# Keys and values in token order "four to a partition" in a windowed attention with a routed expert layer

## The chip, the cores and the metric

The kernel runs on one core of a Trainium2 chip. The metric is the time of one execution on the device in microseconds (us); the median of several runs is compared. The engines are named as the profile names them: PE (TensorE matmuls; PEld its weight loads), DVE (VectorE), ACT (ScalarE), POOL (GpSimd) and SP (SyncE, which here only issues transfers). A "q" behind an engine's name is its instruction queue.

## The reference, cut to what matters

There are 8 batches, 8 heads, 512 local tokens of width 64 and 32 global tokens. A local token sees the 32 global tokens and the local ones within 32 positions; a global token sees all 544. The result, 4352 tokens of 512 numbers, goes through a dense layer of 8 experts whose weights come from a Sinkhorn normalisation.

```python
k_all = np.concatenate([k_g, k_l], axis=2)
out_g = np.matmul(sm(scale * np.matmul(q_g, k_all.transpose(0, 1, 3, 2))), v_all)
mask = np.abs(pos[:, None] - pos[None, :]) <= 32
s_ll = np.where(mask, scale * np.matmul(q_l, k_l.transpose(0, 1, 3, 2)), -1e9)
s_l = np.concatenate([scale * np.matmul(q_l, k_g.transpose(0, 1, 3, 2)), s_ll], axis=-1)
out_l = np.matmul(sm(s_l), np.concatenate([v_g, v_l], axis=2))
...
P = np.exp(logits)                 # logits = x @ w_gate, less their maximum
for _ in range(8):
    P /= P.sum(1, keepdims=True) + 1e-09
    P /= P.sum(0, keepdims=True) + 1e-09
    P *= N / E
for e in range(E):
    out += P[:, e:e + 1] * (np.maximum(x @ w1[e], 0.0) @ w2[e])
```

## The kernel before

**Stages.** The first stage is attention, about the first 265 us; then the Sinkhorn normalisation; then the experts. The order of the instructions on each engine is written out by hand: what the loop emits first runs first on its engine, and each engine works in order. Matmuls of expert 0 are put between the attention's matmuls by `fill(n)`, which takes n pieces from a queue.

**The attention loop** (L429) has 35 iterations. Iteration i works on several head pairs p at once (p counts batch x 4 head pairs; one half batch of four heads is two consecutive p):

- `stage_ak(p = i)` (L282): four PE transposes turn the keys `k16` of two heads into `kTw`, four blocks of 128 tokens, each with 32 global columns, 32 columns of the block on its left and 32 of the block on its right. A DVE copy (L290) takes the transposed keys from PSUM; three POOL copies add the global columns (L291) and the two neighbours' edges (L293, L294).
- `stage_aq(p = i)` (L296): eight PE transposes (L304), four for each head, into two PSUM tiles; ACT copies the first head's rows to `qTz`, DVE the second's (L306). Each head has its own `qTz` whose other 64 rows stay zero.
- `stage_b(p = i - 1)` and `stage_e`: scores (L320, PE), mask and row minimum in one DVE instruction (L324, from PSUM to `st`, with `nm`), exponential on ACT (L334). SP then issues a transposing transfer `uT<-u` (L338), one for each head.
- `stage_c(p = i - 2)`: PE multiplies `uT` with the values, `va` for the block's own tokens (L350) and `vb` for global and neighbouring ones (L351); DVE divides by the row sum (L354, L357).
- `stage_d(p = i - 3)`: transposes back into `xT` (L365, L366).
- In even iterations the 32 global queries of a half batch: `global_scores` (L373, L381, L385) and on POOL `global_norm` (L392, `ug`); in odd ones `global_turn` and `global_out` (L398, L413).

PSUM tiles named `pt` take turns in two buffers, in the order in which they are asked for.

**Token order.** Queries are loaded with four consecutive tokens to a partition (1 KB in a row of the source), so a transposed block holds every fourth token and the copy to `qTz` puts it in order. Keys are loaded block by block, one token to a partition (256 bytes in a row), by four transfers a half batch (`load_k`, L190). Values come one token to a partition too, for two heads by each transfer (`load_va`, L196).

**Who issues which transfer.** POOL issues keys, queries, values and expert weights, and converts fp32 to fp16 on the way. At the end of an even iteration i it issues the keys of two blocks, the queries and values; at the end of an odd one the keys of the other two blocks and values. These are wanted from iteration i + 2 on (`n = i // 2 + 1`, L481). `q16` and `k16` have two buffers. SP issues the edges of `vb` (`load_vb_edges`, L202 and L203, which copy rows of `va` and so wait for its transfers), the global rows of `vb` (L208), the `uT` transfers and, in the first iterations of the second half, some small loads. POOL and SP too work in order: a transfer that waits holds back those behind it.

**The mask** (L229 to L255) is made once: the row order is changed by four transfers to fit the queries' order; three variants serve inner, first and last blocks.

Of the kernel before, what the change touches and what calls it, by code (L numbers as in the profile page):

```python
# [17 lines left out]
P = 128  # L18
NEG = -1.0e9
# [3 lines left out]
def kernel(  # L23
# [124 lines left out]
    with ExitStack() as actx:  # L148
# [24 lines left out]

        def new_qk(k):
            q16 = ain.tile([P, 4, NJ * Dh], FP16, tag="q16", name=f"q16_{k}")
            k16 = ain.tile([P, NJ, 4, Dh], FP16, tag="k16", name=f"k16_{k}")
            qk[k] = (q16, k16)
            return q16, k16

        def q_src(k):  # L180
            b, half = divmod(k, 2)
            return q_l[b, 4 * half : 4 * half + 4].rearrange("h (p s) d -> p h (s d)", s=NJ)

        def k_src(k, so):
            b, half = divmod(k, 2)
            return k_l[b, 4 * half : 4 * half + 4, P * so : P * (so + 1)].rearrange("h p d -> p h d")

        def load_k(k, sos):
            for so in sos:
                nc.gpsimd.dma_start(out=qk[k][1][:, so], in_=k_src(k, so))  # L190

        def load_q(k):
            nc.gpsimd.dma_start(out=qk[k][0], in_=q_src(k))  # L193

        def load_va(b, x):
            nc.gpsimd.dma_start(out=va_buf[b % 2][:, 2 * x : 2 * x + 2, :, 0:Dh].rearrange("p h j d -> p (h j) d"),  # L196
                                in_=v_l[b, 2 * x : 2 * x + 2].rearrange("h (j p) d -> p (h j) d", p=P))

        def load_vb_edges(b, x):
            va, vb = va_buf[b % 2], vb_buf[b % 2]  # L200
            h = slice(4 * x, 4 * x + 4)
            nc.sync.dma_start(out=vb[Sg : Sg + WIN, h, 1:NJ], in_=va[P - WIN : P, h, 0 : NJ - 1])  # L202
            nc.sync.dma_start(out=vb[Sg + WIN : Sg + 2 * WIN, h, 0 : NJ - 1], in_=va[0:WIN, h, 1:NJ])  # L203
# [10 lines left out]
        sk = stage(28, 2).rearrange("p a (b h d) -> p (a b) h d", h=4, d=Dh)  # L214
        sq = stage(30, 2).rearrange("p a (b c) -> p (a b) c", c=NJ * Dh)
# [3 lines left out]
        for so in range(NJ):  # L219
            nc.sync.dma_start(out=sk[:, so], in_=k_src(0, so))  # L220
        nc.scalar.dma_start(out=sq, in_=q_src(0))
# [15 lines left out]
        load_va(0, 0)  # L237
        load_va(0, 1)
# [15 lines left out]
        for s in range(NJ):  # L254
            nc.sync.dma_start(out=mask[Q4 * s : Q4 * (s + 1)], in_=mnat[s:P:NJ])  # L255
# [375 lines left out]
```

## Time and profile before

| | us |
|---|---|
| median of 3 runs (lowest, highest) | 1129.17 (1126.85, 1130.38) |
| profiled execution, its own time | 1128.02 |
| its span | 1126.2 |
| PE busy (share of the span) | 1063.0 (94%) |
| DVE busy | 567.9 (50%) |
| ACT busy | 327.2 (29%) |
| POOL busy | 206.0 (18%) |

The profile's page lists for each engine its busy time, a picture of the span in 40 slices, the chain of waits that ended last, and the costliest groups of instructions. A group's line gives the source line, engine, operation, what is written from what with shapes, how often; then its total busy time and the mean in ns; then the idle time just before it and what ended that. "Issue" lines give transfers, their size and the median time from issue to landing. PE's busy time counts pipelined matmuls and is no measure of its peak. The mean granted clock of TensorE was 0.985 of full speed.

### The profile page before, as it was taken

To read this page: it belongs to the slowest core of one execution; us is meant where nothing else is said; L and a number is where in the kernel's file an instruction comes from. 1 tells how busy PE (TensorE), PEld (TensorE's weight loads), DVE (VectorE), ACT (ScalarE), POOL (GpSimd) and SP (SyncE) were. 2 spreads that over 40 slices of the span, in tenths; PEclk is the share of its full clock that TensorE was granted. 3 is DMA by queue.
4 is the path that set the end of the run, shared out by engine and by line. 5 is a ranking of instruction groups with operands and counts; after the bars stand their busy time and mean duration, and the time that the engine had idled before them with its cause. 6 is when DMAs were issued, how large, how long until landed. Compare 5 with 4: busy or idle time off the path is not lost.

```text
span 1126.2 us, 16517 instructions
## 1 busy us (share of the span) xinstructions
PE 1063.0 (94%) x6394; PEld 539.2 (48%) x6394; DVE 567.9 (50%) x1388; ACT 327.2 (29%) x675; POOL 206.0 (18%) x291
## 2 busy tenths in 40 slices
PE   3598898889999999999999999999999999999998
PEld 2455555555544454445444544445444544454444
DVE  5678787877724444444444444444444444444443
ACT  4466666655421121111111111112111111111111
POOL 6655455541097000000000000000000000000000
PEclk9689999999999999999999999999999999999999
DMA  9999999995102231001300040004000400002222
GB/s 149 158 163 146 130 122 134 134 123 105 18 1 42 34 53 23 1 1 19 57 1 1 1 75 1 1 1 75 1 1 1 76 1 1 1 1 76 75 75 93
DMA packets 181950, 60.97 MB, mean 54 GB/s; under 512 B 156912, under 2 KB 173424, under 8 KB 181872
## 3 DMA queue, kind: packets, MB, share of 16 engines
q0 software_dynamic: 89184, 29.25, 26.9%
q1 hardware_dynamic: 92160, 30.15, 15.6%
q8 instruction: 50, 0.82, 0.3%
q10 hardware_dynamic: 528, 0.52, 0.1%
q14 instruction: 28, 0.23, 0.1%
HBM read 60.57 MB, written 8.91 MB: 62 GB/s over the span
## 4 chain that ended last, share of the span: by engine, by line
PE 82%; DMA 7%; DVE 4%; POOL 3%; issue 2%; ACT 1%; POOLq 0%; DVEq 0%; SPq 0%; ACTq 0%
PE py L115 39%; PE ph L95 38%; DMA k<-in_k_l_dram 4%; DMA uT<-u 2%; POOL k L190 1%; DVE st L324 1%; PE s L320 1%; PE pq L304 1%; POOL va L196 1%; DVE out_nat L123 1%; DMA kgs<-in_k_g_dram 1%; POOL ug L392 0%; PE pog L413 0%; POOL q L193 0%; DVE gm L381 0%
## 5 line engine op out<-in xcount | busy, mean ns | idle before, releaser
L95 PE MATMUL ph<-xT,w1e 128*128 128x512 f16 (+1 forms) x2304 | 500.0, 368 | 0.3 <-DVE P_nat L425 0.3
L115 PE MATMUL py<-w2e,ht 128*128 128x512 f16 x2176 | 497.2, 379 | 0.0
L102 ACT ACTIVATE ht<-ph 128x512 f16<-128x512 f32 (+1 forms) x336 | 192.3, 572 | 687.0 <-PE ph L95 686.5
L95 PEld LDWEIGHTS <-w1e 128*128 128x128 f16 x2304 | 223.1, 98 | 220.5 <-issue 0.9
L115 PEld LDWEIGHTS <-ht 128*128 128x128 f16 x2176 | 210.7, 98 | 232.5 <-ACT ht L102 0.5
L125 DVE SCALAR_TENSOR_TENSOR out_nat<-py,P_nat,out_nat 128x512 f32<-128x512 f32 x238 | 178.7, 751 | 248.1 <-PE py L115 247.2
L104 DVE TENSOR_SCALAR ht<-ph 128x512 f16<-128x512 f32 (+1 forms) x240 | 158.4, 660 | 226.4 <-PE ph L95 225.6
L334 ACT ACTIVATE u<-st,nm 128x224 f16<-128x224 f32 x256 | 105.8, 472 | 55.3 <-DVE nm L324 35.9
L72 POOL DMA_DIRECT2D w1e<-in_moe_w_dram x7 | 5.4, 767 | 510.1 <-PE ph L95 505.0
L324 DVE CUSTOM_DVE_ANT_0 st<-s,mask 128x224 f32<-128x224 f32 x256 | 85.1, 385 | 7.5 <-PE s L320 4.0
L320 PE MATMUL s<-kTw,qTz 128*128 128x224 f16 x256 | 47.8, 275 | 22.6 <-DVE nm L324 19.6
L589 POOL TENSOR_SCALAR out_nat<-out_nat,P_nat 128x512 f32<-128x512 f32 x32 | 49.6, 1561 | 35.7 <-DVE P_nat L586 35.7
L190 POOL DMA_DIRECT2D k<-in_k_l_dram x62 | 47.7, 776 | 0.1
L320 PEld LDWEIGHTS <-qTz 128*128 128x128 f16 x256 | 23.4, 103 | 45.0 <-issue 30.7
L392 POOL TENSOR_SCALAR ug<-ug,gr 128x544 f16<-128x544 f16 x16 | 26.2, 1638 | 29.5 <-DVE gr L391 29.5
L196 POOL DMA_DIRECT2D va<-in_v_l_dram x32 | 29.2, 916 | 0.0
L289 PE MATMUL pk<-identity,k 128*128 128x128 f16 x128 | 16.6, 235 | 11.0 <-DMA k<-in_k_l_dram 10.7
L350 PE MATMUL po<-va,uT 128*128 128x65 f16 x256 | 22.0, 200 | 5.2 <-DMA uT<-u 5.1
L293 POOL COPY kTw<-kTw 128x96 f16<-128x96 f16 x32 | 9.0, 280 | 87.5 <-DVE kTw L290 87.4
L350 PEld LDWEIGHTS <-uT 128*128 128x128 f16 x256 | 19.4, 102 | 9.3 <-DMA uT<-u 5.7
L304 PEld LDWEIGHTS <-q 128*128 128x128 f16 x256 | 19.6, 108 | 7.6 <-issue 1.4
L304 PE MATMUL pq<-identity,q 128*128 128x128 f16 x256 | 22.9, 238 | 0.4 <-DVE kTw L290 0.2
(100 smaller groups left out, 429.6 us busy)
## 6 DMA issues: line engine op xcount, KB each, us to landing
w1e<-in_moe_w_dram POOLq DMA_DIRECT2D x8, 1024.0 KB, 8.0
w2e<-in_moe_w_dram POOLq DMA_DIRECT2D x8, 1024.0 KB, 10.4
out_dram<-out_nat SPq DMA_DIRECT2D x32, 256.0 KB
va<-in_v_l_dram POOLq DMA_DIRECT2D x32, 128.0 KB, 7.5
k<-in_k_l_dram POOLq DMA_DIRECT2D x62, 64.0 KB, 4.9
q<-in_q_l_dram POOLq DMA_DIRECT2D x15, 256.0 KB, 5.9
vb<-va SPq DMA_DIRECT2D x32, 49.5 KB
vb<-vg SPq DMA_DIRECT2D x32, 33.0 KB
```

What stands on the lines that cost most here:

```text
L95: nc.tensor.matmul(ph[:, 0:N], w1e[:, dk, P * fm : P * (fm + 1)], xT[:, dk, P * t0 : P * t0 + N], start=(dk == 0), stop=(dk == DP - 1))
L102: nc.scalar.activation(out=ht[:, 0:N], in_=ph[:, 0:N], func=AF.Relu)
L104: nc.vector.tensor_scalar(out=ht[:, 0:N], in0=ph[:, 0:N], scalar1=0.0, scalar2=None, op0=ALU.max)
L115: nc.tensor.matmul(py, hT[fk][:, P * c : P * (c + 1)], w2e[:, fk, :], start=(fk == 0), stop=(fk == FT - 1))
L125: nc.vector.scalar_tensor_tensor(out=out_nat[:, t, :], in0=py, scalar=P_nat[:, t, e : e + 1], in1=out_nat[:, t, :], op0=ALU.mult, op1=ALU.add)
L190: nc.gpsimd.dma_start(out=qk[k][1][:, so], in_=k_src(k, so))
L304: nc.tensor.transpose(pt[:, s, :], q16[:, c0 : c0 + P], identity)
L320: nc.tensor.matmul(ps[:, jj, 0:KW], qTz[:, P * j : P * (j + 1)], kTw[:, j, :], start=True, stop=True)
L324: nc.vector.tensor_tensor_reduce(out=st[:, jj, :], in0=ps[:, jj, 0:KW], in1=mask[:, mvar[j], :], scale=-scale, scalar=3.0e38, op0=ALU.add, ...
L334: nc.scalar.activation(out=u[:, j, 0:KW], in_=st[:, jj, :], func=AF.Exp, scale=-1.0, bias=nm[:, jj : jj + 1])
L350: nc.tensor.matmul(o, uT[:, 2 * j, :], va[:, 2 * hp + hi, j, 0:W], start=True, stop=False)
L589: eng.tensor_scalar(out=out_nat[:, t, :], in0=out_nat[:, t, :], scalar1=P_nat[:, t, 0:1], scalar2=None, op0=ALU.mult)
```

## The change

Keys are loaded like the queries, four consecutive tokens to a partition, by one transfer a half batch into a raw tile; the queries go into a raw tile too. One iteration later POOL copies both into the order (token within four, head, width). A transposed block of keys then holds every fourth token, and within each block of 128 the columns of `kTw` are kept as four runs of 32; the DVE copy from PSUM, the edge copies, the mask's columns and the rows of `va` and `vb` follow that order. Values therefore come in four transfers a batch, each to 32 partitions and for all eight heads, and the edges of `vb` in four and four transfers of eight partitions. The queries of two heads need only four transposes; ACT makes both copies to `qTz`. Raw and ordered tiles have one buffer each. In the first iterations some work changes place: the first half batch is cast in two parts, all values of batch 0 are loaded ahead of the loop, and `qgP`, `vb` and `vg` are set up in other iterations.

```diff
-        def load_k(k, sos):
-            for so in sos:
-                nc.gpsimd.dma_start(out=qk[k][1][:, so], in_=k_src(k, so))
-        def load_q(k):
-            nc.gpsimd.dma_start(out=qk[k][0], in_=q_src(k))
-        def load_va(b, x):
-            nc.gpsimd.dma_start(out=va_buf[b % 2][:, 2 * x : 2 * x + 2, :, 0:Dh].rearrange("p h j d -> p (h j) d"),
-                                in_=v_l[b, 2 * x : 2 * x + 2].rearrange("h (j p) d -> p (h j) d", p=P))
+        def src_of(x, k):
+            b, half = divmod(k, 2)
+            return x[b, 4 * half : 4 * half + 4].rearrange("h (p s) d -> p h (s d)", s=NJ)
+        def load_qk(k):
+            raws[k] = tuple(ain.tile([P, 4, NJ * Dh], FP16, tag=t, bufs=1, name=f"{t}_{k}") for t in ("qr", "kr"))
+            for dst, x in zip(raws[k], (q_l, k_l)):
+                nc.gpsimd.dma_start(out=dst, in_=src_of(x, k))
+        def order_qk(k):
+            for dst, src in reversed(list(zip(new_qk(k), raws.pop(k)))):
+                nc.gpsimd.tensor_copy(out=dst, in_=src.rearrange("p h (s d) -> p s h d", s=NJ))
+        def load_va(b, s):
+            nc.gpsimd.dma_start(out=va_buf[b % 2][Q4 * s : Q4 * (s + 1), :, :, 0:Dh].rearrange("p h j d -> p (h j) d"),
+                                in_=v_l[b].rearrange("h (j p s) d -> s p (h j) d", p=Q4, s=NJ)[s])
...
+        def load_vb_left(b):
+            va, vb = va_buf[b % 2], vb_buf[b % 2]
+            for s in range(NJ):
+                nc.sync.dma_start(out=vb[Sg + W8 * s : Sg + W8 * (s + 1), :, 1:NJ],
+                                  in_=va[Q4 * (s + 1) - W8 : Q4 * (s + 1), :, 0 : NJ - 1])
...
-            nc.vector.tensor_copy(out=kTw[:, :, 0:P], in_=pt)
+            loc = kTw[:, :, 0:P].rearrange("d j (s p) -> d j s p", s=NJ)
+            nc.vector.tensor_copy(out=loc, in_=pt.rearrange("d s (j p) -> d j s p", j=NJ))
...
-            for hi, copy in ((0, nc.scalar.copy), (1, nc.vector.tensor_copy)):
-                pt = ps_t.tile([P, NJ, P], FP16, tag="pt", name=f"pq{p}_{hi}")
-                for s in range(NJ):
-                    c0 = ((lh + hi) * NJ + s - hi) * Dh
-                    nc.tensor.transpose(pt[:, s, :], q16[:, c0 : c0 + P], identity)
+            pt = ps_t.tile([P, NJ, P], FP16, tag="pt", name=f"pq{p}")
+            for s in range(NJ):
+                nc.tensor.transpose(pt[:, s, :], q16[:, s, lh : lh + 2, :], identity)
+            for hi in range(2):
                 r = slice(Dh * hi, Dh * (hi + 1))
-                copy(out=qTz_buf[2 * (p % NQ) + hi][r].rearrange("d (j s p) -> d j s p", j=NJ, s=NJ),
-                     in_=pt[r].rearrange("d s (j p) -> d j s p", j=NJ))
+                nc.scalar.copy(out=qTz_buf[2 * (p % NQ) + hi][r].rearrange("d (j s p) -> d j s p", j=NJ, s=NJ),
+                               in_=pt[r].rearrange("d s (j p) -> d j s p", j=NJ))
...
                 if i % 2 == 0:
-                    new_qk(n)
-                    load_k(n, (0, 1))
-                    load_q(n)
-                if i == 0 or i % 2 == 1:
-                    load_k(n, (2, 3))
+                    load_qk(n)
+                else:
+                    order_qk(n)
             x, bv = (i + 3) % 4, (i + 3) // 4
...
+            elif bv < B:
+                if x < 2:
+                    load_va(bv, 2 * x)
+                    load_va(bv, 2 * x + 1)
+                    load_vb_globals(bv, (2 * x, 2 * x + 1))
+                elif x == 2:
+                    load_vb_left(bv)
+                else:
+                    load_vb_right(bv)
```

## The prediction

> **What bounds the kernel now.** I read the page's slices first, then stretches of the trace, then the chain in order of time.
>
> ```profile
> PE   3598898889999999999999999999999999999998
> PEclk9689999999999999999999999999999999999999
> DMA  9999999995102231001300040004000400002222
> ```
>
> Each digit is 1/40 of the span, 28 us. From slice 10 on TensorE is full with expert matmuls and the transfers are nearly idle: nothing there is touched. The change lives in the first 265 us, the attention stage, where PE has gaps and the DMA engines are over 90% busy. PE's order is fixed when the kernel is built, so each microsecond that attention ends earlier or later moves the end by as much.
>
> Two consecutive pairs of iterations, by stretches (columns PE, PEld, DVE, ACT, POOL busy, clock, DMA share, GB/s):
>
> ```profile
> 186.40:201.84 15.44, 13.75 (x159) 8.95 (x160) 11.69 (x50) 12.02 (x30) 8.59 (x14) 1.00 1.58 132
> 201.84:216.80 14.96, 13.56 (x152) 8.76 (x153) 13.21 (x52) 8.41 (x21) 8.60 (x14) 1.00 1.45 143
> ```
>
> No engine is full; POOL is at 57%. The waits between 130 and 240 us (seven pairs) say what PE lacks (total, times, longest):
>
> ```profile
> PE pk L289 <- DMA k<-in_k_l_dram: 7.3, 8, 2.5
> PE s L320 <- DVE nm L324: 6.6, 14, 1.0
> ```
>
> Keys landing late cost 7.3/7 = 1.05 us a pair, the scores' lag behind VectorE 0.94. The chain shows why keys are late (start, length, what):
>
> ```profile
> 189.31 0.88 POOL ug L392
> ...
> 190.91 1.57 POOL k L190 x2
> 192.48 0.75 POOL q L193
> 193.23 0.89 POOL va L196
> 194.11 0.30 POOL kTw L291
> ...
> 195.47 6.25 DMA k<-in_k_l_dram
> 201.77 0.23 PE pk L289
> ```
>
> The four key loads of one pair are split over two iterations. The last is issued 4 us after the global normalisation (L392, 1.6 us long, over at 190.95) and lands just before 201.77: 10.8 us from that end.
>
> Prices, from the groups and transfer issues of the same 130:240 stretch:
>
> ```profile
> L291 POOL COPY kTw<-kgT 128x128 f16<-128x128 f16 x13 | 4.4, 335 | 0.0
> L293 POOL COPY kTw<-kTw 128x96 f16<-128x96 f16 x14 | 3.9, 280 | 41.5 <-DVE kTw L290 41.5
> L392 POOL TENSOR_SCALAR ug<-ug,gr 128x544 f16<-128x544 f16 x7 | 11.5, 1637 | 9.5 <-DVE gr L391 9.5
> L306 ACT COPY qTz<-pq 64x512 f16<-64x512 f16 x14 | 8.0, 573 | 8.7 <-PE pq L304 8.7
> L306 DVE COPY qTz<-pq 64x512 f16<-64x512 f16 x14 | 6.0, 428 | 1.0 <-PE pq L304 0.4
> ...
> va<-in_v_l_dram POOLq DMA_DIRECT2D x14, 128.0 KB, 7.9
> q<-in_q_l_dram POOLq DMA_DIRECT2D x7, 256.0 KB, 5.7
> ```
>
> How long is a pair? The transposes of iterations 7 and 31 (L289) start at 68.7 and 255.1 us: 24 iterations, 12 pairs, 15.5 us each.
>
> **The change part by part.**
>
> *Keys and queries: load, then reorder on GpSimd.* Removed per pair: four key issues (0.78 us each). Added: one key issue of the queries' shape (0.76 us) and two POOL copies of 128x1024 fp16. No such copy is in the trace. The nearest rows are POOL's own copies: 335 ns for 128 elements and 280 for 96 give 1.72 ns an element, hence T = 335 + 896 x 1.72 = 1.9 us. The low end: the mask's affine selects in the first 10 us, 212 ns for 32 elements and 293 for 128 (0.84 ns each), give 1.05 us. The high end is the rate of L392, 3.0 ns: 3.1 us. I take 1.9, by the same operation's rows.
>
> Counted from the end of L392: queries issue (0.76), keys issue, keys land 5.7 us after, so 6.5. That is the queries' row; those stood behind two short-packet key loads, the keys will stand behind the queries. Ends: 4.4 us, the queries' shortest, and 7.9, the values' row. I take the row of the same shape. The keys are copied at 6.5 + 1.9 = 8.4, where the old keys came at 10.8 and PE asked for them at 9.75. The wait goes, with 1.35 us to spare: -1.05 a pair. Queries are copied at 10.3. PE asked at 202.89, 11.9 after; less the lost wait that is 10.9: hidden by 0.6 us. What is late next is the scores' wait on VectorE, which stays.
>
> *What queues behind the waiting copy on POOL.* It waits for the landing; behind it stand the value loads (every second pair, 2 x 0.92), the three window copies of the next iteration (0.66 from start to end at 194.07) and L392, which releases the next load. So a new loop exists: 0.76 + 5.7 + 2 x 1.9 + 0.66 + 1.64 = 12.6 us, 14.4 with value loads, 13.5 on average. Pairs will last about 14.2, so every second one can lose a little: +0.2 a pair. Single buffers for ordered and raw tiles make the copy wait for the former transposes too; those are over by 195 us, before the landing.
>
> *Query transposes.* Four instead of eight an iteration. Eight take 202.89 to 203.34 on PE, 0.45 us, so 0.45 a pair less work; PE also stands 0.94 a pair waiting for VectorE, so I count -0.25 (ends 0 and -0.45).
>
> *Copies.* DVE loses 2 x 0.43 a pair, ACT gains 2 x 0.57: from (12.02 + 8.41)/2 = 10.2 to 11.4 of some 14 us. What hides it is ACT's wait for these transposes (8.7 us in seven pairs); uncovered it would cost 1.15 x 12 = 14 us. The gain on DVE I count at nothing (to -0.86 a pair). Window copies with shorter runs and the key copy in another order (L306's 428 ns has that pattern; L290 took 420) cost 0.0 to 0.1 us a pair on POOL and DVE: hidden in POOL's slack, +1 us in all if not.
>
> *Values in four quarters of 32 partitions, edges in eight issues instead of four a batch.* SP issues 4 x 0.59 = 2.4 us more in a batch's 31 us, and it waits for the last quarter with the score transposes (L338) queued behind it; stage C on PE needs those. Now SP loses 11.4 us in the seven pairs to such waits and PE doesn't wait for uT between 80 and 260 us. Hidden; without cover 2.4 x 7 batches = 17 us.
>
> *Start.* The mask gets three more small DVE copies (at most 0.6 us by the 0.57 us copy at 6.37); its transfer starts at 9.98, DVE is done at 7.1: hidden. Two value loads move into POOL's 2.7 us idle before 10.5, three key issues go, so the q_g load, which is in the chain (18.49, 4.09 us), can start up to 4 us earlier; but it then stands behind more value bytes, and 17 us of uT waits follow at 34.7 to 54.6. Weights issued behind a reorder at iterations 3 and 5 come some 7 us later; L115 first needs them at 76 us. I take -1, ends -4 and +2.
>
> Sum: 12 x (-1.05 - 0.25 + 0.2) - 1 = -14 us. The profiled run took 1128.0 (span 1126.2): 1114. The median of the runs is 1.2 above it: **1115 us**.
>
> *Two rules against the trace.* POOL's short copies run at 1.72 ns an element here. The Trainium skill, GPSIMD Engine Reference, "Elementwise — side-by-side cycle accounting", has 1.8 cycles an element at 1.2 GHz for a tight one-input loop and 2.6 for two inputs: an estimate of 1.5 to 2.2 us for T; at 2.2 the loop averages 14.1, 15.0 with value loads; the 0.2 becomes 0.6 and the sum -9. Second, POOL's 96-element copies last 266 to 298 ns from 60 to 260 us, whatever DVE does. SBUF — State Buffer, "Who interferes with whom", speaks against long POOL copies: a DVE instruction that uses both of its ports shuts GpSimd out for its whole length. In this stage DVE reads PSUM, which that rule leaves free; if it applied, an estimate of up to 0.7 us (xn's length) for each reorder would add 1.4 a pair and make the sum +3.
>
> **The rivals.**
>
> 1. *GpSimd's loop becomes the bound (slower).* The copies run at L392's rate, 3.1 us. Then queries are ready at 6.5 + 6.2 = 12.7, 1.8 after PE asks, and the loop is 0.76 + 5.7 + 6.2 + 0.92 + 0.66 + 1.64 = 15.9 on average, 16.8 with value loads: +0.4 a pair, or +1.3 if short pairs can't make up for long ones, 12 x 0.4 to 12 x 1.3: 1133 to 1144. It decides where the landing and two copies together pass 11.5 us, which brings the loop to 15.5: T = 2.9 at a landing of 5.7, T = 1.8 at 7.9. For it: L392, the only long POOL arithmetic here. Against it: the short copies' slope, and fewer packets in the queue.
> 2. *Everything is hidden and the copies are fast* (T near 1.1). The loop is 12 us, the wait and all of the 0.45 go, and DVE's lighter load shortens the scores' wait by 0.2: 12 x -1.7 - 2 = -22: 1107. For it: the affine selects' slope. Against: DVE stands between matmuls anyway.
> 3. *Score transposes come late.* SP's longer wait and eight edges take uT's slack; PE waits 2 to 2.4 us a batch: -14 + 15 = about +1: 1130. For it: SP stands before L338 now. Against: no uT wait in 180 us.
> 4. *ACT takes the wait's place*: half of the 14 us uncovered gives -7: 1122.
>
> **How the numbers follow.** Forecast 0.42, rival 2 0.18, rival 4 0.14, rival 3 0.07 (half of it within 0.3%), rival 1 0.19. A difference under 0.3% (3.4 us) can't be told from none. Faster: 0.42 + 0.18 + 0.13 = 0.73, less 0.02 for mixtures: 0.71. Same: 0.06. Slower: 0.23. The forecast's own range is 1109 to 1121. For 8 in 10: down to 1104, below rival 2, and up to 1136, into rival 1's lower half.
>
> **What would show it.** Right: no wait of pk on a key transfer; POOL's 128x1024 copies under 2.5 us; pairs of 14 to 14.4 us; q0's packets fewer by a third; ACT's query copies twice as many. Wrong: pq or pk waiting for POOL, window copies late before L320, L350 waiting for uT, or VectorE's lag growing beyond 0.94 a pair.

## The result and the profile after

| | before | after |
|---|---|---|
| median (lowest, highest), us | 1130.35 (1126.85, 1132.79) | 1143.01 (1132.38, 1147.5) |
| ratio of after to before | | 1.0108, 95% interval 1.0085 to 1.0131 |
| profiled execution, us | 1128.02 | 1136.88 |
| its span, us | 1126.2 | 1135.1 |

The change makes the kernel about 12 us slower; 1115 was forecast, and 1143 lies outside the range. Only the attention stage moves: the key transposes of iterations 7 and 31 start 186.4 us apart before and 196.1 after, so a pair of iterations takes 16.3 us instead of 15.5, and these 9.7 us are more than the 8.9 us between the spans.

The page of after: the slices, queue q0, what the engines' costliest groups waited for, and the loads.

```profile
PE   3587888779999999999999999999999999999997
...
DMA  9999999993300413000400040004000400002222
...
q0 software_dynamic: 64368, 29.11, 21.6%
...
PE 80%; DMA 13%; DVE 3%; ACT 2%; issue 1%; SPq 1%; POOL 0%; DVEq 0%; ACTq 0%; POOLq 0%
...
L363 PE MATMUL po<-va,uT 128*128 128x65 f16 x256 | 23.8, 200 | 35.8 <-DMA uT<-u 35.7
...
L191 POOL COPY k<-kr 128x1024 f16<-128x1024 f16 x15 | 15.6, 1040 | 51.8 <-DMA kr<-in_k_l_dram 47.8
...
va<-in_v_l_dram POOLq DMA_DIRECT2D x32, 128.0 KB, 5.2
qr<-in_q_l_dram POOLq DMA_DIRECT2D x15, 256.0 KB, 5.2
kr<-in_k_l_dram POOLq DMA_DIRECT2D x15, 256.0 KB, 6.7
```

Much of what was forecast happened: q0 has 28% fewer packets, GpSimd's copies take 1.04 us, no key transpose on PE waits for a transfer. But the chain now holds 13% of transfers (7% before), and the value matmuls on PE, which waited 5.1 us for `uT` in the whole run before, wait 35.7.

The waits of the same stretch as in the prediction, 130 to 240 us, PE's first:

```profile
PEld L363 <- DMA uT<-u: 14.1, 9, 3.6
PE po L363 <- DMA uT<-u: 12.9, 8, 3.5
...
PE s L333 <- DVE nm L337: 4.5, 9, 1.6
```

No pk line with a key transfer is left (7.3 us before); in its place stand 12.9 us of the value matmuls waiting for `uT`, a wait that before did not have here at all. SP's queue:

```profile
SPq L351 <- ACT u L347: 48.1, 16, 5.8
SPq L351 <- ACT qTz L319: 12.0, 7, 2.1
...
SPq L202 <- DMA va<-in_v_l_dram: 0.6, 1, 0.6
```

SP no longer waits for values (0.6, before 11.4); the score transposes (L351) wait for ScalarE's exponentials, and in 7 of them the last thing in front was a query copy. From 60 to 280 us, by line, the weight loads and the products of after's value matmuls (counted together, though the waits of the two overlap) stood idle for `uT`:

```profile
  DMA uT<-u: 51.9, 30
```

Before it was 0.2. The page's stretch by pairs (iterations 18 to 23; columns as in the prediction):

```profile
157.76:173.44 15.68, 13.07 (x151) 8.48 (x150) 10.97 (x49) 12.88 (x30) 8.18 (x13) 1.00 1.20 120
173.44:188.30 14.86, 12.68 (x135) 8.10 (x134) 12.02 (x50) 9.88 (x23) 8.26 (x13) 1.00 1.05 137
188.30:204.71 16.41, 13.06 (x151) 8.47 (x149) 10.89 (x49) 12.88 (x29) 8.18 (x13) 1.00 1.35 124
```

PE is busy for 12.9 us of a pair on average, 0.7 less than in the two pairs shown before, and yet the pairs are longer (15.65 against 15.2 us). The chain of after from 162 us on shows what fills them:

```profile
162.42 0.37 ACT u L347
162.80 0.03 issue
162.82 13.21 DMA uT<-u x2
176.03 0.47 ACT qTz L319
176.50 0.02 issue
176.52 0.58 ACT qTz L319
177.10 0.03 issue
177.13 0.86 ACT u L347 x2
177.99 0.02 issue
178.01 6.42 DMA uT<-u
184.43 0.05 issue
184.48 0.20 PE po L363
```

Two query copies, the last exponentials, a transfer of 6.4 us, the value matmuls: a chain in which PE only comes at the end. GpSimd's order of time in the same place:

```profile
160.82 1.64 POOL L405 TENSOR_SCALAR ug<-ug,gr 128x544 f16<-128x544 f16 x1 [0.81 <-DVE gr L404]
162.42 0.82 POOL L187 DMA_DIRECT2D qr<-in_q_l_dram  x1
163.24 0.76 POOL L187 DMA_DIRECT2D kr<-in_k_l_dram  x1
163.99 1.57 POOL L194 DMA_DIRECT2D va<-in_v_l_dram  x2
```

SP issues the even iteration's second `uT` in between, and PE needs it in the odd iteration that follows, where the waits stand:

```profile
162.82 1.23 SPq L351 DMA_TRANSPOSE uT<-u  x1
```

Within 3.2 us, 512 KB of queries and keys and two value loads are queued, and the first of them ahead of that `uT`. Before, at the same place (iteration 22), the order was the other one: the first keys were queued at 190.91, and `uT` had gone out 0.9 us earlier:

```profile
189.97 1.24 SPq L338 DMA_TRANSPOSE uT<-u  x1
```

**How far uT was from being late.** A `uT` transfer adds to its semaphore sixteen times, and it has landed with the last of these: the 6.42 us from 178.01 in the chain above are such a flight. The trace also holds single packets, 1024 of 256 bytes in queue q1 for each `uT`, in the order of issue, so the first can be told. Means over the nine even iterations 12 to 28 for the second head, in us from the iteration's first key transpose (where PE waited for the landing, the value matmul started 0.05 us after it):

| kernel | issued | flight | landed | first head's value matmuls | second head's | PE's wait there |
|---|---|---|---|---|---|---|
| before | 4.71 | 2.90 | 7.61 | 11.54 | 11.78 | 0 |
| after | 4.79 | 7.42 | 12.21 | 9.88 | 12.26 | 1.97 |

PE wants the second head 0.24 us after the first. So before, PE asked at 11.78 for what was there at 7.61: a slack of 4.2 us. After, PE asks at 10.12, 1.66 us earlier, mostly because the iteration lost its key wait and half of its query transposes: that is the gain itself. The landing is 4.6 us later. The two together, 6.3, are 2.1 more than the slack, and PE waits 2.0. Of the longer flight 1.95 us are the time to the first packet (1.21 to 3.16), 2.6 the time from there to the landing (1.69 to 4.26). In the odd iterations it was the other way round: there the second head's flight was 7.96 us before, with only 0.89 us of slack, and is 5.52 after, with 2.95.

**What moved is the loads.** SP issues that `uT` as late as before (4.79 against 4.71). But before, all nine went out 0.8 to 1.3 us ahead of the first load of their iteration (1.04 on average), and landed after 2.7 to 2.9 us, one after 3.95. After, all nine go out 0.4 to 1.0 us behind it (0.69), and land after 6.4 to 9.1. The loads stand behind the normalisation (`ug`), and that waits for a reciprocal on VectorE (`gr`) which stood right behind VectorE's query copy. Without that copy the reciprocal is over at 2.39 us instead of 4.04, and all that GpSimd does behind it comes earlier too.

### The profile page after: what moved, and what is told of

Same layout as the page of the kernel before. It is cut to its first block, busy times and chain, and to the rows that moved or that the text cites. A ratio compares the mean times of both kernels' runs of the same rounds, so it can differ in the third digit from the quotient of the medians.

```text
span 1135.1 us, 16317 instructions
## 1 busy us (share of the span) xinstructions
PE 1055.6 (93%) x6266; PEld 532.8 (47%) x6266; DVE 555.2 (49%) x1361; ACT 348.3 (31%) x708; POOL 198.9 (18%) x274
## 3 DMA queue, kind: packets, MB, share of 16 engines
q1 hardware_dynamic: 90576, 30.15, 15.5%
## 4 chain that ended last, share of the span: by engine, by line
PE 80%; DMA 13%; DVE 3%; ACT 2%; issue 1%; SPq 1%; POOL 0%; DVEq 0%; ACTq 0%; POOLq 0%
PE ph L95 38%; PE py L115 38%; DMA uT<-u 11%; ACT u L347 1%; DMA va<-in_v_l_dram 1%; PE s L333 1%; DVE st L337 1%; ACT qTz L319 1%; DVE gm L394 1%; DMA out_nat<-in_v_g_dram 1%; PE po L363 1%; PE sa L386 0%; PE po L364 0%; SPq L202 0%; DMA mask<-out_nat 0%
## 5 line engine op out<-in xcount | busy, mean ns | idle before, releaser
L363 PE MATMUL po<-va,uT 128*128 128x65 f16 x256 | 23.8, 200 | 35.8 <-DMA uT<-u 35.7
L600 POOL TENSOR_SCALAR out_nat<-out_nat,P_nat 128x512 f32<-128x512 f32 x32 | 49.6, 1561 | 35.7 <-DVE P_nat L597 35.7
L319 ACT COPY qTz<-pq 64x512 f16<-64x512 f16 x64 | 36.9, 576 | 14.0 <-PE pq L316 13.2
L367 DVE RECIPROCAL rc<-po 128x8 f32<-128x8 f32 x32 | 6.6, 206 | 51.0 <-PE po L364 51.0
L194 POOL DMA_DIRECT2D va<-in_v_l_dram x32 | 25.1, 792 | 2.8 <-PE s L333 2.2
L191 POOL COPY k<-kr 128x1024 f16<-128x1024 f16 x15 | 15.6, 1040 | 51.8 <-DMA kr<-in_k_l_dram 47.8
L364 PE MATMUL po<-vb,uT 128*128 128x65 f16 x256 | 23.8, 199 | 0.0
L370 DVE TENSOR_TENSOR xn<-po,rc 128x512 f16<-128x512 f32 x32 | 22.1, 691 | 1.1
```

What stands on the lines that cost most here:

```text
L319: nc.scalar.copy(out=qTz_buf[2 * (p % NQ) + hi][r].rearrange("d (j s p) -> d j s p", j=NJ, s=NJ), in_=pt[r].rearrange("d s (j p) -> d j s ...
L363: nc.tensor.matmul(o, uT[:, 2 * j, :], va[:, 2 * hp + hi, j, 0:W], start=True, stop=False)
L600: eng.tensor_scalar(out=out_nat[:, t, :], in0=out_nat[:, t, :], scalar1=P_nat[:, t, 0:1], scalar2=None, op0=ALU.mult)
```

## The experiments

Ratios are to the kernel before, run beside it on the same chip; one point is 1% (11.3 us). The changed kernel stands at +1.1 points.

| run | from | edit | median, us | ratio (95%) |
|---|---|---|---|---|
| e1 | after | second query copy on VectorE | 1126.77 | 0.9972 (0.9952 to 0.9993) |
| e2 | after | both loads moved to the odd iteration | 1129.05 | 0.9964 (0.9947 to 0.9981) |
| e3 | after | no GpSimd copies, loads write the order | 1145.51 | 1.0131 (1.0091 to 1.0171) |
| e4 | after | four more edge transfers a batch | 1159.66 | 1.0233 (1.0192 to 1.0274) |
| e5 | after | last exponentials ahead of the query copies | 1126.24 | 0.9967 (0.9932 to 1.0002) |
| e6 | after | e2 and e1 | 1121.0 | 0.9898 (0.9863 to 0.9932) |
| e7 | after | e2 and e5 | 1115.68 | 0.9848 (0.981 to 0.9886) |
| e9 | after | edges issued by GpSimd | 1138.01 | 1.01 (1.0055 to 1.0145) |
| e10 | after | e2, e5 and e1 | 1143.25 | 1.0137 (1.0107 to 1.0166) |
| b1 | before | both query copies on ScalarE | 1133.62 | 1.0024 (1.0001 to 1.0047) |
| b2 | before | all key loads at the even iteration's end | 1127.03 | 0.9981 (0.9959 to 1.0003) |
| b3 | before | b1 and b2 | 1129.81 | 0.9978 (0.9954 to 1.0003) |
| f1 | after | values and edges as before | 1137.45 | 1.0101 (1.0059 to 1.0142) |
| f2 | before | values and edges as after | 1134.12 | 1.0062 (1.0031 to 1.0094) |
| f3 | before | b3 and f2 | 1136.69 | 1.0075 (1.004 to 1.0109) |
| f4 | after | no GpSimd copies, raw tiles read | 1148.24 | 1.0193 (1.0154 to 1.0232) |
| f5 | after | each load in four parts | 1129.18 | 1.0007 (0.9975 to 1.0039) |
| f6 | after | e5, and the keys' load alone moved | 1117.15 | 0.9892 (0.9858 to 0.9926) |

### ScalarE's copies, the moment of the loads, the packets (e1, e2, e3, b1)

```diff
# e1
-                nc.scalar.copy(out=qTz_buf[2 * (p % NQ) + hi][r]...
+                (nc.scalar.copy, nc.vector.tensor_copy)[hi](out=qTz_buf[2 * (p % NQ) + hi][r]...
# e2
-                if i % 2 == 0:
+                if i == 0:
                     load_qk(n)
-                else:
+                elif i % 2 == 1:
                     order_qk(n)
+                    if n + 1 < 2 * B:
+                        load_qk(n + 1)
# e3: q16 and k16 with two buffers, no order_qk
+                src = x[b, 4 * half : 4 * half + 4].rearrange("h (p s) d -> p s h d", s=NJ)
+                nc.gpsimd.dma_start(out=dst, in_=src)
# b1, in the kernel before
-            for hi, copy in ((0, nc.scalar.copy), (1, nc.vector.tensor_copy)):
+            for hi, copy in ((0, nc.scalar.copy), (1, nc.scalar.copy)):
```

> The changed kernel with one thing undone: the second head's query copy is back on VectorE. After the change PE waits for uT at the start of stage C (PE and its weight loads name uT in 30 waits between 60 and 280 us; 12.9 us of PE time in seven pairs) and ScalarE makes its two query copies (0.58 us each) just before the last exponentials that release the transfer. Theory ACT (the second copy makes uT late): each of the 32 transfers goes 0.58 us earlier, the wait in odd iterations falls by about as much, some 9 us in all: about 1134. Theory BURST (the transfer is slow because query and key loads are issued at the same moment): the wait hardly falls, VectorE's work grows by 0.43 us an iteration: 1140 to 1146. Theory SP (edge issues hold the queue): unchanged, 1143.

> The changed kernel with the query and key loads of the next half batch issued at the end of odd iterations, right behind the reorder that frees the raw tiles, instead of at the end of even ones. Theory BURST: the second head's transfer of even iterations (issued at 162.8, landed 6.8 us later, where the old kernel's comparable ones took about 2.4 us) no longer meets the loads and lands in 3 us or so; the iteration from the odd key transposes to the even ones falls from about 8.9 back towards 7.5 us, 16 times 1.4 = 22 us: 1118 to 1125. Theory ACT: the issue is as late as before, the time stays within 4 us of 1143. Theory SP: the same, 1143.

> The changed kernel without the reorder on GpSimd: the loads of queries and keys at the end of even iterations write the ordered tiles directly (two buffers each), in runs of 64 numbers, so 256-byte reads and 128-byte writes instead of 1024 and 512, four times as many packets. Theory BURST with long packets (a transfer's packets take turns with the load's, and a 512-byte packet holds an engine about twice as long as a 128-byte one): a transposing transfer beside the burst lands in about 4.5 instead of 6.8 us and the time falls to 1128 to 1136. Theory BURST by sheer load time (four times the packets, some 5 us of all engines for each half batch instead of 2.5): the wait stays or grows, 1143 to 1160. Theory ACT or SP: 1143.

> The kernel before with one part of the change alone: both query copies on ScalarE (still eight transposes in two PSUM tiles). Theory ACT: uT goes 0.58 us later in each iteration, and the old kernel has little slack there, so stage C begins to wait for uT: 1134 to 1140 against 1130. Theory BURST or SP: hidden, within 3 us of 1130, as the prediction counted it.

e1 and e2 each take back 1.4 points, and both part `uT` from the loads. In e2 the even iteration's second `uT` flies 5.16 us instead of 7.42: 2.8 to 4.7 where nothing is queued beside it, and still 6.4 to 8.4 in the four iterations that queue two value loads 0.4 us ahead of it. e2 misses the 1118 to 1125 us of its theory by 4 us. e1 is faster than all three of its theories expected, and not by an earlier issue: `uT` goes out at 4.84 us, as late as in after. VectorE's copy holds the reciprocal back to 3.86 us, the first load is queued 0.8 us behind `uT` on average, and the flight is 5.04, beside an even iteration that is 0.7 us longer. In the kernel before, both copies on ScalarE (b1) cost a quarter of a point: that `uT` is issued 0.66 us later (5.37), now 0.3 us behind the first load, and flies 4.65, still inside the slack. e3 has the burst and the copies with 256-byte reads, and no reordering on GpSimd: 1.3 points slower than before, flight 6.50 us, 51.2 us of `uT` waits from 60 to 280 us. Long packets are not needed for the loss.

### Edges, and the exponentials first (e4, e5, e6, e7)

```diff
# e4
                 elif x == 2:
                     load_vb_left(bv)
+                    load_vb_left(bv)
# e5 (e7 has this and e2's edit; e6 has e1's and e2's)
             fill(1)
+            if Bs:
+                stage_e(pb, 1, 1)
             if A:
                 stage_aq(pa)
             if ks is not None:
                 global_norm(ks, gsu.pop(ks))
             fill(1)
-            if Bs:
-                stage_e(pb, 1, 1)
```

> The changed kernel with the four left-edge transfers of each batch issued twice: 4 x 0.78 = 3.1 us more on SP's queue a batch (0.78 is the step between two of them in the changed kernel's chain), ahead of the transposing transfers of the next even iteration. Theory SP (the extra edge issues make uT late): seven batches times up to 3.1 = 22 us more, 1155 to 1165. Theories ACT and BURST: SP mostly waits for ScalarE's exponentials (some 60 of 110 us), so at most a third of it shows: 1143 to 1150.

> The changed kernel with one change of order: the last exponentials of the second head stand ahead of the query transposes and of ScalarE's two query copies, so uT goes out about 1.2 us earlier. With the second copy back on VectorE alone (0.58 us earlier) the time fell from 1143 to 1127. Theory ACT, refined (what counts is how late uT is issued against a landing time of 2.3 to 8 us): 1.2 us earlier gives as much or more, 1114 to 1127. Theory BURST: the transfer still meets the loads unless it gets out ahead of them; at most half of it, 1130 to 1143. Third possibility, that VectorE's or ScalarE's load and not the order made the difference in that run: no change, 1143.

> The changed kernel with both single steps together: loads at the end of odd iterations, second query copy back on VectorE. Alone they gave 1129 and 1127. If they are two separate causes of the same wait (a late issue and a slow landing), they add until the wait is gone: of 40 us of uT waits in the changed kernel some 30 go, 1110 to 1120. If both do the same thing, that is keep the transfer and the loads apart in time, they don't add: 1124 to 1130.

> The changed kernel with loads at the end of odd iterations and the last exponentials ahead of the query copies; both copies stay on ScalarE. If the uT wait is all that the change cost, what is left is the gain that was forecast for the rest (no wait for keys, four transposes fewer): 1108 to 1118. If ScalarE's added 1.2 us an iteration pair costs something of its own, 1120 or more.

Four more edge issues a batch (0.77 us each on SP) cost 1.25 points, 14 us: once the slack is gone, what stands on SP ahead of `uT` is paid. (In e4's profile the granted clock between 80 and 280 us was 0.92, in after's 0.98, so a part of the 14 us may be slower matmuls.) e5 issues the even iteration's second `uT` at 4.18 instead of 4.79 us and gains 1.4 points. It shows both orders in one kernel: in iterations 14, 18, 22 and 26 `uT` now goes out 0.8 us ahead of the first load and lands after 2.7 to 4.0 us; in the other five the load is still 0.4 to 1.6 us ahead, and it takes 7.2 to 8.0. With the loads moved as well (e7) the time is 1115.7 us, 1.5 points faster than before, and 2.6% faster than the changed kernel (0.9848 / 1.0108 = 0.974). From iteration 12 on its pairs take 14.2 us (15.7 before, 16.3 after), and the waits between 130 and 240 us begin with

```profile
POOL kTw L308 <- DVE kTw L303: 39.6, 15, 4.9
ACT u L347 <- DVE nm L337: 11.2, 11, 1.8
...
PE s L333 <- ACT qTz L319: 4.4, 7, 0.8
PE s L333 <- DVE nm L337: 4.3, 8, 1.0
```

with PE waiting for VectorE and the query copies, and only once, for 1.3 us, for `uT`. Everything that the forecast counted on is in this kernel. (Over iterations 7 to 31 its pairs take 14.7 us, where the forecast's sum had 14.4.) e6, which puts the second copy on VectorE instead, is half a point behind, 1 us above its expected range: VectorE waits 11.0 us for ScalarE's copy in the same stretch.

### What three edits together do, the edges on another queue, the burst in the old kernel (e9, e10, b2, b3)

```diff
# e9, in both edge functions
-                nc.sync.dma_start(out=vb[...
+                nc.gpsimd.dma_start(out=vb[...
# b2
-                    load_k(n, (0, 1))
+                    load_k(n, range(NJ))
                     load_q(n)
-                if i == 0 or i % 2 == 1:
-                    load_k(n, (2, 3))
```

> The changed kernel with all edge transfers of vb issued on GpSimd's queue instead of SP's, in the same places of the program. Four edges issued in a row hold SP for 3.1 us; issuing four more a batch cost 17 us in the run with doubled edges. Theory SP (the eight edge issues a batch, ahead of the transposing transfers, carry a good part of the loss): uT goes up to 3 us earlier in two of four iterations, and the time falls by 8 to 17 us, 1126 to 1135, although GpSimd now spends some 6.4 us more a batch. If the edges cost only where their number passes SP's slack, which eight do not: 1140 to 1150.

> The changed kernel with loads at the end of odd iterations, the last exponentials ahead of the query transposes, and the second query copy on VectorE. With the first two alone 1115.7 was measured; there scores now wait for ScalarE's query copies (13 us in 15 waits of PE). If those waits are on the path, halving them gives 1108 to 1113. If VectorE's 0.43 us an iteration is worth as much (its lag behind the scores is the other wait that is left), 1114 to 1121.

> The kernel before with one part of the change's timing alone: all four key loads of a half batch are issued at the end of the even iteration, with the queries and values, in the old packets and the old token order. The wait of pk on keys (about 1.05 us a pair) must go, since the last key load is issued some 4 us earlier: -12 us if nothing takes its place, 1118. Theory BURST (loads at that moment slow the second head's transfer of even iterations): uT waits of 1 to 2 us appear in odd iterations and eat the gain, 1126 to 1136. If the long packets are needed for that: 1116 to 1122.

> The kernel before, with both suspected causes put in and nothing else of the change: both query copies on ScalarE (0.24% slower alone) and all four key loads together with the queries at the end of the even iteration (0.19% faster alone, where the key wait, worth some 12 us, went and 17 us of waits for uT came). Eight query transposes, the old value loads and the four old edges stay, GpSimd copies nothing. Theory (uT is late because it is issued behind ScalarE's copies and flies beside the burst): the two add up or worse, 1134 to 1145 us, with over 25 us of waits of PE for uT in the whole span and most of them in odd iterations. Rival (the loss in the changed kernel needs its value loads, edges or GpSimd copies): 1127 to 1132 us, under 20 us of waits for uT.

Taking the edges off SP gains 0.1 point, less than the interval, and 1138.0 us lies between its two expected ranges; what the edges cost on GpSimd instead isn't told apart. e10 was to be the best and is 2.9 points worse than e7. Between 130 and 240 us PE has no wait for `uT` there; the waits show another engine:

```profile
DVE qTz L319 <- ACT qTz L319: 19.1, 13, 2.0
...
POOL ug L405 <- DVE gr L404: 17.6, 6, 3.0
PE s L333 <- DVE nm L337: 15.3, 13, 1.9
```

VectorE's copy and ScalarE's read the same PSUM tile and run one after the other. With the exponentials ahead of ScalarE's copy, VectorE stands up to 2.0 us for it, and the scores, the key transposes and the normalisation stand behind VectorE. The change's one tile for both heads thus makes ScalarE for both copies the better choice, once `uT` has slack.

b2 is the old kernel with the burst. The key wait is gone, 13.1 us of `uT` waits appear between 60 and 280 us, and 0.2 points are left, an interval that still reaches no gain. b3 has burst and copies and, against the theory, costs nothing either: 19.5 us of such waits, and no key wait. So the two suspects alone do not rebuild the loss. In b3 the second `uT` is issued at 4.90, 0.8 us behind the first load, and still flies only 4.86 us, not 7.42; PE asks at 11.2, not 10.1. Two questions followed: what else of the change lengthens the flight, and whether values, edges or GpSimd's copies do it.

### Values, edges and GpSimd's copies (f1, f2, f3, f4)

```diff
# f1: after, with load_va(b, x), load_vb_edges(b, x) and their places in the loop as before
# f2: before, with load_va(b, s), load_vb_left, load_vb_right and their places as after
# f3: f2 with the edits of b1 and b2
# f4: after, raw tiles with two buffers
+            qk[k] = tuple(t_.rearrange("p h (s d) -> p h s d", s=NJ) for t_ in raws[k])
...
-                else:
-                    order_qk(n)
```

> The changed kernel, but values and edges are loaded as before: one transfer of two heads in each iteration, four edge transfers a batch (the rows of the values are then not in the order of the scores' columns; the work is the same). Theory V (the new value loads and edges are what makes the burst and ScalarE's copies cost more here than in the kernel before): 1118 to 1129 us, under 30 us of waits for uT between 60 and 280 us (51.9 in the changed kernel). Rival C (GpSimd's copies are): still 1137 to 1146 us and over 40 us of such waits.

> The kernel before with the new value loads and edges alone: quarters of 32 partitions, two in every first and second iteration of four, and four and four edge transfers (rows not in the order of the scores' columns; the work is the same). Theory V: slower, 1134 to 1148 us, with over 15 us of waits for uT between 60 and 280 us (0.2 before). Rival C: 1126 to 1132 us.

> The kernel before with all three: new value loads and edges, both query copies on ScalarE, all key loads at the end of the even iteration (rows of the values not in the order of the scores' columns; the work is the same). The former run with the last two alone took 1129.8 us with 19.5 us of waits for uT between 60 and 280 us. Theory V: 1140 to 1155 us, over 40 us of such waits. Rival C: 1128 to 1133 us.

> The changed kernel without GpSimd's two copies a pair: the transposes read 128 neighbouring columns of the raw tiles, which have two buffers (the reordering of keys and queries is left out, the work of the other engines is the same). Theory V: 1137 to 1147 us, over 40 us of waits for uT. Rival C: 1118 to 1130 us, under 30 us of them.

Neither theory holds. With the old values and edges the changed kernel loses as much (f1: 46.0 us of `uT` waits, flight 7.07). The new ones cost the kernel before 0.6 points (f2), and 1.0 on top of b3 (f3), with only 4.8 and 25.4 us of `uT` waits. In f2 the flight of the even iterations is no longer than before (2.73) and PE waits for keys there, 8.8 us between 130 and 240; how the new value loads make its pairs longer was not followed further. In f4 the transposes read two runs of 64 columns in the raw tiles, not 128 neighbouring ones as its expectation has it, so the order is kept; `uT` waits are 54.1 us. Without GpSimd's copies the changed kernel is 0.9 points slower, not faster: nothing then holds the value loads of the odd iteration back until the keys have landed. That this is why was not tested.

### The rate at which loads are queued (f5, f6)

b3 and f1 differ in how the same bytes are queued: by their rows the four key loads and the queries take GpSimd 3.9 us to issue (2 x 1.57 and 0.76), the two whole loads 1.6.

```diff
# f5
-            for dst, x in zip(raws[k], (q_l, k_l)):
-                nc.gpsimd.dma_start(out=dst, in_=src_of(x, k))
+            for h in range(4):
+                for dst, x in zip(raws[k], (q_l, k_l)):
+                    nc.gpsimd.dma_start(out=dst[:, h], in_=src_of(x, k)[:, h])
# f6: e5's edit, and
+                if i == 0:
+                    load_raw(n, "kr", k_l)
                 if i % 2 == 0:
-                    load_qk(n)
+                    load_raw(n, "qr", q_l)
                 else:
                     order_qk(n)
+                    if n + 1 < 2 * B:
+                        load_raw(n + 1, "kr", k_l)
```

> The changed kernel with each of the two loads of a pair issued in four parts of one head (64 KB each, the same bytes and packets, eight issues of some 0.76 us in place of two). In the changed kernel the second head's uT of an even iteration is issued 4.8 us after that iteration's first key transpose, as before (4.7), but flies 6.3 us (3.7 before); in the kernel before with the four key loads and the queries behind one another it flew 4.5. Theory (what slows uT is that two transfers of 256 KB are queued within 1.5 us): that flight falls under 5.2 us and the waits for uT between 60 and 280 us under 40 us; keys land later, so 1128 to 1142 us. Rival (it is the long packets, or something other than the rate of issue): flight still 5.8 us or more, waits over 46 us, 1140 us or more.

> The changed kernel with the last two exponentials ahead of ScalarE's query copies, and the burst parted: the keys' load moves to the end of the odd iteration behind GpSimd's copies, the queries' stays at the end of the even one. Theory (two 256 KB transfers at once slow uT): each is harmless by itself, under 12 us of waits for uT between 60 and 280 us, 1108 to 1116 us, at least as fast as with both loads moved (1115.7). Rival (any load issued there is as bad): over 20 us of waits, 1120 to 1128 us.

f5 changes nothing but the number of issues: the same bytes, packets, copies and edges. Its GpSimd in order of time, at the same place:

```profile
160.44 0.61 POOL L188 DMA_DIRECT2D qr<-in_q_l_dram  x1
161.06 0.55 POOL L188 DMA_DIRECT2D kr<-in_k_l_dram  x1
...
164.20 0.59 POOL L188 DMA_DIRECT2D kr<-in_k_l_dram  x1
164.72 1.65 POOL L195 DMA_DIRECT2D va<-in_v_l_dram  x2
```

The eight parts take 4.3 us to queue (the three flights that f5's expectation compares, 6.3, 3.7 and 4.5, are 7.42, 2.90 and 4.86 to the landing), and the value matmuls' waits for `uT` from 60 to 280 us fall to

```profile
  DMA uT<-u: 13.6, 9
```

The even iteration's second `uT` flies 4.80 us, its first packet comes after 1.60 us, although the first part is queued 0.4 us ahead of it on average. The kernel is 1.0 points faster than the changed one, although its key transposes now wait for GpSimd (5.2 us between 130 and 240, where the keys' last part lands later). The expected time and flight are met, and the rival's are not. Each part is also smaller than a whole load, so f5 shows what parting does and not whether size or spacing does it. f6 parts the burst in two places: flight 3.92 us and pairs of 14.0 us from iteration 12 on. One load alone is not harmless: queued within 0.4 us of `uT` it makes it 4.2 to 5.7 us, queued 0.8 us behind it 2.7 to 3.7. At 1117.15 us it misses its expected range by 1 us, and its 16.3 us of `uT` waits are above the 12 expected; its time agrees with e7's within the intervals.

In the table the first load is counted from the issue of `uT` (negative: ahead of it); e2 and e7 queue only value loads there, in four of the nine iterations.

| kernel | issued | first load | flight | landed | PE's wait there | pair, iterations 12 to 29 |
|---|---|---|---|---|---|---|
| before | 4.71 | 1.04 | 2.90 | 7.61 | 0 | 15.7 |
| b3 | 4.90 | -0.79 | 4.86 | 9.76 | 0 | 15.2 |
| after | 4.79 | -0.69 | 7.42 | 12.21 | 1.97 | 16.3 |
| f5 | 4.64 | -0.44 | 4.80 | 9.44 | 0.08 | 14.9 |
| e5 | 4.18 | -0.08 | 5.59 | 9.78 | 0.83 | 15.1 |
| e2 | 4.78 | -0.40 | 5.16 | 9.94 | 0.75 | 15.5 |
| f6 | 3.66 | 0.44 | 3.92 | 7.57 | 0 | 14.0 |
| e7 | 3.58 | 0.81 | 4.42 | 8.00 | 0.15 | 14.2 |

The order at the issue is not all: in e7 the four with value loads 0.8 us behind them still take 4.5 to 8.1 us. Why was not followed.

## Why the prediction was wrong

*The gains were there.* The key wait of 1.05 us a pair went in full. The even iteration, from its first key transpose to the next, fell from 7.91 to 6.74 us in after, as the sum of key wait and query transposes asks; in f6 and e7 the odd one fell too, from 7.81 to 7.3 and 7.4. With `uT` freed by two edits (e7) the kernel takes 1115.7 us; the forecast was 1115. That the two agree so closely is partly luck: the exponentials' new place is none of the change's parts, and whether it would speed up the kernel before was not run.

*T, the copy of 128x1024, was taken at 1.9 us and is 1.04.* The mask's selects (0.84 ns an element) were the right neighbours, not POOL's own short copies. By the rows of after, 270 ns for 96 elements and 1040 for 1024, the fixed part of such a copy is 190 ns and an element takes 0.83 ns; the slope between two short copies of different kind had made it 1.72. The prediction's estimate from the Trainium skill, GPSIMD Engine Reference, "Elementwise — side-by-side cycle accounting", 1.5 us at the least, was too high as well: the measurement decides. The rule on VectorE's ports (SBUF — State Buffer, "Who interferes with whom") shows in no row: after's copies of keys and queries average 1040 and 1041 ns between 130 and 240 us.

*The landing was taken at 5.7 and is 6.7 for the keys,* inside its ends. With the smaller T the reorder is still in time, and the GpSimd loop, the +0.2 and rival 1, never bound.

*The start* was taken as -1: the transposes of iteration 7 start at 67.7 instead of 68.5 us.

*The step that failed is "PE doesn't wait for uT between 80 and 260 us. Hidden; without cover 2.4 x 7 batches = 17 us",* and with it the copies' "What hides it is ACT's wait for these transposes". Both named a cover and neither measured how thick it was. A wait of nothing says only that the slack is not below zero; the trace gives it as 4.2 us for the second head of the even iterations. The forecast gain alone takes 1.66 of that, since PE comes to `uT` earlier while SP issues it as late as before (4.79 against 4.71 us). What was left, 2.5 us, was overspent by a term that was not in the sum at all: the effect of the new loads on someone else's transfer. The prediction priced when queries and keys land and nothing that flies beside them, although the change moves the loads of a pair from 1.0 us behind the even iteration's second `uT` to 0.7 us ahead of it. That flight grew by 4.5 us. A part of the move comes from a term that was put at nothing, "The gain on DVE I count at nothing": the copy that VectorE lost had held back the normalisation and with it the loads, and e1, which gives it back, has the loads 0.8 us behind `uT` again. f5 shows the loads' part: the same loads, queued over 4.3 us instead of 1.6, bring the flight to 4.8 us and give back 1.0 points.

*What it costs in the sum:* 2.0 us of wait in each pair, 24 us over 12 pairs. With that the sum of -14 becomes +10; the profiled executions differ by +9, the medians by +13. From iteration 12 on the pairs of f6 and e7 are 2.2 and 2.0 us shorter than after's, 24 to 27 us over 12 such pairs; their medians are 26 and 27 us lower.

*The copies on ScalarE* cost a quarter of a point in the kernel before (b1), and the second of them 1.4 in the changed one (e1). The price of 14 us "uncovered" was near in size, but not as time of ScalarE: the copies stand ahead of the exponentials that release `uT` (e5), and without the copy on VectorE the loads come earlier. The cover was the slack of `uT`, not ScalarE's wait for the transposes.

*The edges on SP* gain 0.1 point when GpSimd issues them (e9), so they were hidden or nearly so, unless GpSimd lost what SP gained. Four more of them cost 14 us (e4), near the 17 for no cover.

*The rivals.* Rival 3 had the place right, score transposes late, and its mechanism wrong: SP's edges were to eat the slack, at 1130 us with a chance of 0.07. Rival 4 had ScalarE's share. Rival 2 comes nearest to e7 in mechanism (fast copies, all hidden) but its 1107 us was not reached. Rival 1 has the result in its range, 1133 to 1144, by luck: its loop does not exist.

*What stays open.* The slack is shared, so its users' prices don't add: f5, e2, e5 and e1 alone each give back 1.0 to 1.4 points, e2 and e5 together 2.6. Why the new value loads and edges slow the kernel before (f2), and why the changed kernel is slower without GpSimd's copies (f4), was not settled.

## What to carry to other kernels

Before a step is costed at nothing because nobody waits for it, measure its slack: the time from landing to first use, in every phase of the loop, less what the change itself takes by making the consumer come earlier. When loads are moved or merged, or an engine that releases them is relieved, ask which transfer that something waits for starts in the same microseconds, whether it goes out ahead of the loads or behind them, and price that one, not only the loads. A load that nobody needs soon can be issued in parts (f5, 1.0 points) or in the other iteration (e2, 1.4); with the transfer issued earlier as well it was 2.6 (e7).

## What the runs showed of the hardware

- A score transpose (128x1024 fp16, SBUF to SBUF) has at its best landed 2.7 us after SP starts to issue it (in f2 all nine took 2.71 to 2.74). Issued 0.4 to 1.0 us behind the first of two loads of 256 KB that are queued within 1.6 us, it took 7.4 on average. Of the 4.5 us between before and after 1.95 lie ahead of its first packet and 2.6 behind it. The Trainium skill, DMA: Bandwidth & Descriptors, "Queues, rings and completion order", says that an engine takes turns between queues, a packet from each. Turns would stretch what lies behind the first packet; these runs don't show how much of it they are, nor where the transfer stands in the time ahead of the first.
- How the same bytes are queued matters: in eight parts with the same packets (f5) the flight was 4.8 us. Packet size isn't told apart from that: e3's short packets gave 6.5, but its two loads take GpSimd 2.4 us to issue and after's 1.6.
- GpSimd copies 128x1024 fp16 with a permutation in 1.04 us, 1.0 ns an element, a third of what `ug`'s multiplication by a per-partition scalar takes (1637 ns for 544, 3.0 ns).
- Copies on ScalarE and VectorE that read two halves of one PSUM tile ran one after the other in e1 and e10, so splitting them over two engines held the second engine up to 2.0 us. Whether the chip or the program's own order makes them do so was not told apart.
